# Second layer by seven products per pair: whole-block weight conversion and another order of products in a step

## The chip, the cores and the metric

The kernel runs on one core of one Trainium2 chip. The core has five engines that run side by side, each with its own queue worked off in order: PE (TensorE, matmuls into PSUM), DVE (VectorE), ACT (ScalarE), POOL (GpSimd), and SP (SyncE), which here only issues DMAs. The metric is the device time of one execution in microseconds (us); the median of several runs counts.

## What is computed

```
attn_out = _attn_ref(q, k, v)              # rotary attention, 2 x 8 heads, 576 x 64
x = attn_out as (1152 tokens, 512)
x = elu(x @ w_in) @ w_out                  # first layer,  512 -> 2048 -> 512
h = x @ w_in2                              # second layer, 512 -> 2048
g = h * tanh(log(1 + exp(h)))              # Mish
out = g @ w_out2                           # 2048 -> 512
```

The weights reach the chip in double precision (two 32-bit words per number) and are turned into single precision there. All matrix products are done in three parts: each operand is split into a high part and a low part, and high x high, low x high and high x low are summed.

## The kernel before

The change lies in the second layer alone (`second`, `pair_step`, `last_step`, `out_sum`). The 2048 hidden columns are 16 blocks of 128, taken as 8 pairs q = 0 to 7. Pair 0 is done the plain way (`classic`, three blocks of 384 tokens). For each later pair the first product (x @ w_in2) is done with seven half-size products instead of eight, numbered as in the table `P`: `x.mm(k)` issues product k, 12 matmuls of 288 columns. Products 1, 6, 7, 4 sum one after the other in PSUM bank "a", product 2 goes to bank "b", products 5 and 3 to bank "c"; between them ACT copies the bank's state out (`x.copy`), and DVE adds banks to the copies (`x.add`, L1068, and `x.add22`, L1072). `x.act` applies Mish and writes the high part of g (L1082, L1083, ACT), `x.lo` and `last_lo` the low part (L1086, DVE). The operands t1 to t4 of products 5, 6, 7, 4 are differences of token blocks, formed once at the layer's start on DVE (`form`, L886) and split by `put_hi` (ACT, L909) and `put_lo` (DVE, L913). Product 6 adds to what product 1 left in bank "a", so it can start only when ACT has copied "m1" out of it.

A step q (1 to 6, `pair_step`; 7, `last_step`) does four things at once:

- PE: the seven products of pair q, and nine output blocks (`out_mm`, L1122, six matmuls of 512 columns each) of pair q - 1. An output block goes to one of two PSUM buffers `ps_h`.
- DVE: nine sums (`out_sum`, L1132), each adding an output block to Y and freeing its buffer. For pair 0 it is ACT that copies the block to Y (L1130).
- Weights in: `w` is the two input blocks of pair q + 1, `o` the two output blocks of pair q, `on` those of pair q + 1. `load` makes ACT take the upper words (L92, a tile `wv` for input blocks, `wu` for output blocks); `bits` are three DVE operations (L103, L107, L111) that need the raw block; after the third the raw buffer is free. `w.sums` forms four differences of the input blocks (L820, DVE). `round` writes the high part on ACT and the low part on POOL (L116, L117), or on DVE where `nc.vector` is given.
- SP: DMAs of raw blocks (512 KB each, L78 and L83). There are three raw buffers. A load is issued as soon as the buffer that it takes is free; the buffers are handed out in the order in which their blocks' last bit operations stand in the program.

The order inside a step is written by hand: `pair_step` is a list of calls, and every engine works off its own part of it in that order. In the old list the three blocks `w[0]`, `o[0]`, `o[1]` are converted interleaved, then comes the first bit operation of `w[1]`, and only behind it the first three sums. PE's order is products 2, 1, 5, 6, three output blocks, products 7, 3, six output blocks, product 4.

Of the kernel before, what the change touches and what calls it, by code (L numbers as in the profile page):

```python
# [13 lines left out]
AF = mybir.ActivationFunctionType  # L14
# [11 lines left out]
def kernel(  # L26
# [11 lines left out]
    nc = tc.nc  # L38
# [812 lines left out]
    def moe(mp, early):  # L851
# [274 lines left out]
        def out_sum():  # L1126
            pair, t, o = banks.pop(0)
            y = Y.rearrange("p (t e) -> p t e", e=DM)[:, t, :]
            if pair.q == 0:
                nc.scalar.activation(out=y, in_=o, func=AF.Copy)  # L1130
            else:
                nc.vector.tensor_tensor(out=y, in0=y, in1=o, op=ALU.add)  # L1132
                if pair.q == NF // 2 - 1:
                    nc.sync.dma_start(out=out[t * 128:t * 128 + 128, :], in_=y)

        def pair_step(x, prev, w, o, on):
            x.mm(2)
            x.mm(1)
            x.mm(5)
            w.load(0)  # L1140
            prev.last_lo()
            x.copy("m1", "a")
            w.bits(0, 0)
            w.load(1)
            x.mm(6)
            out_mm()
            o[0].bits(0)
            out_mm()
            x.add("m1", "b")
            o[0].bits(1)  # L1150
            o[1].bits(0)
            w.bits(0, 1)
            x.copy("u2", "a")
            o[1].bits(1)
            w.bits(0, 2)
            o[1].bits(2)
            out_mm()
            o[0].bits(2)
            x.copy("m5", "c")
            w.bits(1, 0)  # L1160
            out_sum()
            out_sum()
            out_sum()
            x.mm(7)
            x.mm(3)
            o[0].round()
            out_mm()
            w.bits(1, 1)
            w.bits(1, 2)
            out_mm()  # L1170
            out_mm()
            x.copy("u3", "a")
            o[1].round(nc.vector)
            out_sum()
            x.add("u2", "c")
            x.act("m1")
            w.sums(0)
            w.sums(1)
            w.round(0)
            on[0].load()  # L1180
            out_mm()
            w.sums(2)
            out_mm()
            x.lo("m1")
            out_mm()
            out_sum()
            out_sum()
            w.round(1)
            w.sums(3)
            x.add22()  # L1190
            x.act("u2")
            out_sum()
            w.round(3)
            w.round(2)
            x.mm(4)
            out_sum()
            x.act("u3")
            out_sum()
            x.lo("u3")
            x.lo("u2")  # L1200
            x.act("s")
            on[1].load()

        def last_step(x, prev, o):
            prev.last_lo()
            x.mm(2)
            x.mm(1)
            x.copy("m1", "a")
            x.mm(5)
            o[0].bits(0)  # L1210
            o[0].bits(1)
            o[0].bits(2)
            o[0].round()
            x.copy("m5", "c")
            x.add("m1", "b")
            x.mm(6)
            x.copy("u2", "a")
            x.act("m1")
            out_mm()
            out_mm()  # L1220
            o[1].bits(0)
            out_sum()
            x.lo("m1")
            x.mm(3)
            out_sum()
            o[1].bits(1)
            o[1].bits(2)
            o[1].round(nc.vector)
            x.add("u2", "c")
            out_mm()  # L1230
            out_mm()
            x.act("u2")
            out_sum()
            out_sum()
            x.mm(7)
            x.lo("u2")
            x.copy("u3", "a")
            out_mm()
# [12 lines left out]
            out_mm()  # L1251
            out_sum()
            out_sum()

        def second():
            NQ = NF // 2
            x = Pair(0)
            w = ahead_pieces
            x.classic(0)
            w.round(0)  # L1260
            put_hi(0, "t4")
            form(1, "t3")
            form(1, "t2")
            x.classic_act(0)
            x.classic_hi(0)
            x.classic(1)
            w.sums(0, 1, 2, 3)
            w.round(1)
            put_hi(1, "t2")
            x.classic_lo(0)  # L1270
            form(0, "t1")
            form(1, "t1")
            x.classic_act(1)
            x.classic_hi(1)
            put_lo(1, "t2")
            w.round(2)
            x.classic(2)
            x.classic_lo(1)
            put_hi(1, "t3")
            w.round(3)  # L1280
            form(1, "t4")
            put_lo(0, "t4")
            put_hi(0, "t1")
            put_hi(1, "t1")
            put_lo(0, "t1")
            put_lo(1, "t1")
            x.classic_act(2)
            x.classic_hi(2)
            put_hi(1, "t4")
            put_lo(1, "t3")  # L1290
            o = [Block(NF + 2 + j) for j in range(2)]
            for b in o:
                b.load()
            put_lo(1, "t4")
            for q in range(1, NQ):
                prev, x = x, Pair(q)
                queue.extend((prev, t) for t in range(NT // 128))
                if q + 1 < NQ:
                    on = [Block(NF + 2 * q + 2 + j) for j in range(2)]
                    pair_step(x, prev, Pieces(q + 1), o, on)  # L1300
                    o = on
                else:
                    last_step(x, prev, o)
            queue.extend((x, t) for t in range(NT // 128))
            while queue:
                out_mm()
                out_sum()

        psum("ps_g")
        with tc.manual_schedule():  # L1310
# [13 lines left out]
            o = [(x[1:], g2_mm(*x[1:])) for x in pend[:1]]  # L1324
# [100 lines left out]
```

## Time and profile before

| | us |
|---|---|
| runs (3) | 595.06 median, 593.76 to 595.62 |
| profiled execution, time | 597.14 |
| profiled execution, span of the trace | 595.4 |
| PE busy | 551.8 (93%) |
| DVE busy | 426.7 (72%) |
| ACT busy | 313.6 (53%) |
| POOL busy | 226.9 (38%) |

The execution takes 1.74 us more than the span that the trace shows. Attention and the first layer fill the span to 351, pair 0 of the second layer runs to 363.65, and from there to 555.11 the six steps follow; the rest is the last step and the last nine output blocks. The profile's row of the granted PE clock shows 9 tenths or more until then and falls to 6 to 9 in the steps. Busy shares are means over stages with different limits: what the change is worth is read from the stage that it touches, there from the waits of PE.

### The profile page before, as it was taken

Reading aid. Unit: us, or ns where it says so; the run is one execution under the profiler, and the core shown is the slowest. Engines: PE = TensorE matmul, PEld = TensorE weight load, DVE = VectorE, ACT = ScalarE, POOL = GpSimd, SP = SyncE. Lnnn points to the kernel's source line nnn. Section 1 sums busy time; section 2 is a strip of 40 time slices with the busy share of each in tenths; the row PEclk is TensorE's granted clock in tenths of the full one; section 3 lists DMA queues with packets and bytes.
Section 4 is the critical chain, followed back from the end, with each engine's and each line's share of the span. In section 5 each row is a group of like instructions: output and inputs, shape, how many; then the busy total and the mean of one; then the engine's idle time right before and its main releaser. Section 6 shows DMA issues by size and latency. Waiting matters only on the chain.

```text
span 595.4 us, 9057 instructions
## 1 busy us (share of the span) xinstructions
PE 551.8 (93%) x3390; PEld 496.7 (83%) x3390; DVE 426.7 (72%) x663; ACT 313.6 (53%) x557; POOL 226.9 (38%) x206
## 2 busy tenths in 40 slices
PE   7999999999999999999999999597979797888997
PEld 6678888888999999999999998486767677776985
DVE  4667777788879878898867889445656665666664
ACT  3666767686566655445555556282535352525430
POOL 7899998633254443444330112030303040302200
PEclk9999999999999999999999999698999989898999
DMA  8368888762323333233232110402121212111004
GB/s 257 102 166 217 214 211 216 183 176 83 107 70 108 107 107 106 72 106 106 73 105 70 37 36 0 141 1 106 36 107 35 106 37 89 54 61 46 1 0 160
DMA packets 49100, 59.81 MB, mean 100 GB/s; under 512 B 20768, under 2 KB 38944, under 8 KB 48288
## 3 DMA queue, kind: packets, MB, share of 16 engines
q1 hardware_dynamic: 48512, 58.64, 33.1%
q8 instruction: 27, 0.44, 0.3%
q10 hardware_dynamic: 544, 0.59, 0.3%
q14 instruction: 17, 0.14, 0.1%
HBM read 47.51 MB, written 2.36 MB: 84 GB/s over the span
## 4 chain that ended last, share of the span: by engine, by line
PE 66%; DVE 15%; DMA 8%; ACT 5%; issue 3%; POOL 2%; SPq 1%; ACTq 0%; DVEq 0%; POOLq 0%
PE ps_s L207 16%; PE ps_h L1122 13%; PE ps_g L922 13%; PE ps_s L1044 10%; PE ps_s L441 5%; PE psA L548 5%; DMA raw<-in_w_in_dram 4%; PE psT L508 3%; DMA qb<-ql 2%; DVE wu L107 2%; DMA v_t<-in_vp_dram 1%; DVE Y L1132 1%; DMA tab<-in_rope_dram 1%; DVE Y L936 1%; DVE ws L820 1%
## 5 line engine op out<-in xcount | busy, mean ns | idle before, releaser
L448 DVE TENSOR_REDUCE mn<-ps_s 128x1 f32<-128x576 f32 x72 | 53.7, 755 | 25.6 <-PE ps_s L441 24.6
L1132 DVE TENSOR_TENSOR Y<-Y,ps_h 128x512 f32<-128x512 f32 x63 | 42.3, 686 | 35.7 <-PE ps_h L1122 35.4
L1122 PE MATMUL ps_h<-wo0h,gg 128*128 128x512 f32 x144 | 47.6, 413 | 17.4 <-DVE Y L1132 10.1
L1122 PE MATMUL ps_h<-wo0bh,gg 128*128 128x512 f32 x144 | 47.8, 414 | 15.1 <-DVE Y L1132 15.1
L461 ACT ACTIVATE P<-ps_s,mn 128x576 f32<-128x576 f32 x72 | 53.0, 738 | 14.4 <-DVE mn L448 14.1
L1122 PEld LDWEIGHTS ps_h<-wo0h,gg 128*128 128x128 f32 x144 | 26.8, 194 | 25.3 <-DVE Y L1132 11.8
L1122 PEld LDWEIGHTS ps_h<-wo0bh,gg 128*128 128x128 f32 x144 | 27.2, 194 | 23.5 <-DVE Y L1132 17.8
L117 POOL TENSOR_TENSOR wo0l<-wu,wo0h 128x512 fp32r<-128x512 f32 x9 | 13.7, 1519 | 80.8 <-ACT wo0h L116 66.3
L508 PE MATMUL psT<-idn,P 128*128 128x128 f32 x288 | 43.0, 273 | 0.0
L117 POOL TENSOR_TENSOR wo0bl<-wu,wo0bh 128x512 fp32r<-128x512 f32 x8 | 11.7, 1462 | 77.9 <-ACT wo0bh L116 70.4
L107 DVE SCALAR_TENSOR_TENSOR wu<-raw,wu 128x512 int32<-128x512 int32 x50 | 40.2, 804 | 1.2
L528 ACT ACTIVATE pt<-psT 128x512 f32<-128x512 f32 x43 | 25.6, 595 | 22.6 <-PE psT L508 22.5
L548 PE MATMUL psA<-pt,v_t 128*64 128x256 f32 (+1 forms) x240 | 36.1, 401 | 0.6 <-ACT R L493 0.3
L111 DVE SCALAR_TENSOR_TENSOR wu<-raw,wu 128x512 int32<-128x512 int32 x50 | 35.6, 723 | 1.1
L508 PEld LDWEIGHTS psT<-idn,P 128*128 128x128 f32 x288 | 34.7, 141 | 1.9 <-issue 1.5
L254 DVE SCALAR_TENSOR_TENSOR tb<-ta,tb 128x768 f32<-128x768 f32 x22 | 21.5, 976 | 20.2 <-ACT tb L250 20.1
L92 ACT ACTIVATE wv<-raw 128x512 f32<-128x512 f32 x14 | 9.2, 659 | 46.2 <-DMA raw<-in_w_in_dram 46.2
L1064 ACT ACTIVATE ta<-ps_s 128x576 f32<-128x576 f32 x28 | 17.5, 646 | 30.4 <-PE ps_s L1044 30.3
L103 DVE TENSOR_SCALAR wu<-wu 128x512 int32<-128x512 int32 x50 | 31.4, 629 | 0.0
L207 PE MATMUL ps_s<-XH,wi0h 128*128 128x384 f32 x120 | 31.0, 338 | 0.0
L207 PE MATMUL ps_s<-XL,wi0h 128*128 128x384 f32 x120 | 30.6, 335 | 0.0
L207 PE MATMUL ps_s<-XH,wi0l 128*128 128x384 f32 x120 | 30.6, 335 | 0.0
(229 smaller groups left out, 1653.5 us busy)
## 6 DMA issues: line engine op xcount, KB each, us to landing
raw<-in_w_in_dram SPq DMA_DIRECT2D x32, 512.0 KB, 3.7
raw<-in_w_out_dram SPq DMA_DIRECT2D x32, 512.0 KB, 3.6
qk_t<-in_qk_dram SPq DMA_DIRECT2D x6, 1152.0 KB, 5.9
qa<-qh SPq DMA_DIRECT2D x24, 144.0 KB, 3.7
out_dram<-Y SPq DMA_DIRECT2D x9, 256.0 KB, 2.0
ka<-kh SPq DMA_DIRECT2D x12, 144.0 KB, 5.4
ka<-kl SPq DMA_DIRECT2D x12, 144.0 KB, 4.9
qb<-ql SPq DMA_DIRECT2D x12, 144.0 KB, 3.0
```

The source lines that it names most:

```text
L103: nc.vector.tensor_scalar(out=ui, in0=ui, scalar1=3, scalar2=0x7FFFFFF8, op0=ALU.logical_shift_left, op1=ALU.bitwise_and)
L107: nc.vector.scalar_tensor_tensor(out=ui, in0=high, scalar=-0x80000000, in1=ui, op0=ALU.bitwise_and, op1=ALU.bitwise_or)
L111: nc.vector.scalar_tensor_tensor(out=ui, in0=low, scalar=29, in1=ui, op0=ALU.logical_shift_right, op1=ALU.bitwise_or)
L207: nc.tensor.matmul(o[:, j, :CH], lhsT=ws[j][i][:, cc, :], rhs=x[:, cc, t * CH:t * CH + CH], start=(k == 0), stop=(k == 3 * NC - 1),)
L448: nc.vector.tensor_reduce(out=m, in_=psS[u][:, :, :HS], axis=AX.XY, op=ALU.min)
L461: nc.scalar.activation(out=P.rearrange("p (j n) -> p j n", j=2), in_=psS.pop(u)[:, :, :HS], func=AF.Exp, scale=-1.0, bias=mn_t.pop(u), acc ...
L508: nc.tensor.transpose(tv[:, c, :], P[:, k:k + 128], idn)
L548: nc.tensor.matmul(o[64 * h:64 * h + 64, cols], lhsT=v, rhs=rhs, start=(c == 0 and first), stop=(c == 4), skip_group_check=True,)
L922: nc.tensor.matmul(o[:, j, :CH], lhsT=WO[f][w][:, e * 128:e * 128 + 128], rhs=g_part(f, t, i), start=(k == 0), stop=(k == 3 * GF - 1),)
L1044: nc.tensor.matmul(self.o[r][:, u, :H2], lhsT=w[i][:, cc, :], rhs=XO[u][xn][x][:, cc, :], start=(first and n == 0), stop=(last and n == 3 ...
L1122: nc.tensor.matmul(o, lhsT=l, rhs=w, start=(k == 0), stop=(k == 5))
L1132: nc.vector.tensor_tensor(out=y, in0=y, in1=o, op=ALU.add)
```

## The change

- `pair_step` is written in another order. PE: products 1, 2, 6, three output blocks, products 7, 5, two output blocks, product 4, an output block, product 3, three output blocks. DVE: all bit operations of `o[0]` and `o[1]`, then three sums (an `add` between them), then all those of `w[0]` and `w[1]`. The Mish of product 4 (`x.act("s")`) stands before the rounding of `w`. `o[1].round` goes from DVE to POOL, `w.round(3)` (a half block) from POOL to DVE.
- `out_sum` copies pair 0's output blocks on DVE, not on ACT.
- `last_step`: `o[1].round` goes from DVE to POOL.
- `second`: the calls ahead of step 1 are in another order.

```diff
             if pair.q == 0:
-                nc.scalar.activation(out=y, in_=o, func=AF.Copy)
+                nc.vector.tensor_copy(out=y, in_=o)
...
         def pair_step(x, prev, w, o, on):
+            x.mm(1)
             x.mm(2)
-            x.mm(1)
...
-            o[1].round(nc.vector)
...
+            o[1].round()
...
+            w.round(3, nc.vector)
 
         def last_step(x, prev, o):
...
-            o[1].round(nc.vector)
+            o[1].round()
...
-            w.sums(0, 1, 2, 3)
-            w.round(1)
+            w.sums(0, 1, 2)
+            w.round(2)
             put_hi(1, "t2")
             x.classic_lo(0)
+            put_lo(1, "t2")
+            x.classic_act(1)
+            x.classic_hi(1)
+            w.sums(3)
             form(0, "t1")
             form(1, "t1")
-            x.classic_act(1)
-            x.classic_hi(1)
-            put_lo(1, "t2")
-            w.round(2)
+            put_hi(1, "t3")
             x.classic(2)
             x.classic_lo(1)
-            put_hi(1, "t3")
-            w.round(3)
+            w.round(1)
+            put_lo(1, "t3")
             form(1, "t4")
             put_lo(0, "t4")
+            w.round(3)
+            x.classic_act(2)
+            x.classic_hi(2)
             put_hi(0, "t1")
             put_hi(1, "t1")
             put_lo(0, "t1")
             put_lo(1, "t1")
-            x.classic_act(2)
-            x.classic_hi(2)
             put_hi(1, "t4")
-            put_lo(1, "t3")
```

DVE at the head of step 3, before (`gg<-sx` is the low part of the last Mish of the pair before, `wv` an input block, `wu` an output block, `Y<-Y,ps_h` a sum; rows that follow each other and read alike are one row with a count):

```order
L1086 TENSOR_TENSOR gg<-sx,gg 128x2x288
L103 TENSOR_SCALAR wv<-wv 128x512
L103 TENSOR_SCALAR wu<-wu 128x512
L1068 TENSOR_TENSOR ta<-ta,ps_s 128x576
L107 SCALAR_TENSOR_TENSOR wu<-raw,wu 128x512
L103 TENSOR_SCALAR wu<-wu 128x512
L107 SCALAR_TENSOR_TENSOR wv<-raw,wv 128x512
L107 SCALAR_TENSOR_TENSOR wu<-raw,wu 128x512
L111 SCALAR_TENSOR_TENSOR wv<-raw,wv 128x512
L111 SCALAR_TENSOR_TENSOR wu<-raw,wu 128x512 x2
L103 TENSOR_SCALAR wv<-wv 128x512
L1132 TENSOR_TENSOR Y<-Y,ps_h 128x512 x3
```

The same place in the changed kernel:

```order
L1086 TENSOR_TENSOR gg<-sx,gg 128x2x288
L103 TENSOR_SCALAR wu<-wu 128x512 x2
L107 SCALAR_TENSOR_TENSOR wu<-raw,wu 128x512
L111 SCALAR_TENSOR_TENSOR wu<-raw,wu 128x512
L107 SCALAR_TENSOR_TENSOR wu<-raw,wu 128x512
L111 SCALAR_TENSOR_TENSOR wu<-raw,wu 128x512
L1132 TENSOR_TENSOR Y<-Y,ps_h 128x512 x2
L1068 TENSOR_TENSOR ta<-ta,ps_s 128x576
L1132 TENSOR_TENSOR Y<-Y,ps_h 128x512
L103 TENSOR_SCALAR wv<-wv 128x512
L107 SCALAR_TENSOR_TENSOR wv<-raw,wv 128x512
L111 SCALAR_TENSOR_TENSOR wv<-raw,wv 128x512
```

The two output blocks are finished one by one, the three sums stand next, and both input blocks come behind the sums.

DVE in the second half of step 3, before (`ws` and the short `wv` rows are `w.sums`, `gg<-ta,gg` low parts of Mish results):

```order
L1132 TENSOR_TENSOR Y<-Y,ps_h 128x512
L1068 TENSOR_TENSOR ta<-ta,ps_s_4457 128x576
L820 TENSOR_TENSOR ws<-wv 128x256
L820 TENSOR_TENSOR wv<-wv 128x256
L820 TENSOR_TENSOR ws<-wv 128x256
L1086 TENSOR_TENSOR gg<-ta,gg 128x2x288
L1132 TENSOR_TENSOR Y<-Y,ps_h 128x512 x2
```

And in the changed kernel:

```order
L1132 TENSOR_TENSOR Y<-Y,ps_h 128x512
L820 TENSOR_TENSOR ws<-wv 128x256
L820 TENSOR_TENSOR wv<-wv 128x256
L820 TENSOR_TENSOR ws<-wv 128x256
L1086 TENSOR_TENSOR gg<-ta,gg 128x2x288
L1072 TENSOR_TENSOR ta<-ta 128x576
L820 TENSOR_TENSOR ws<-wv,ws 128x256
L1132 TENSOR_TENSOR Y<-Y,ps_h 128x512 x2
L1068 TENSOR_TENSOR ta<-ta,ps_s_4521 128x576
L1132 TENSOR_TENSOR Y<-Y,ps_h 128x512
```

DVE's work between the fourth sum and the next two stays of the same kind; on PE, product 3 now lies between the blocks that these sums serve.

ACT where pair 0 ends and step 1 begins, before (L1103 and L1106 are Mish and high part of pair 0, `XH` and `xt` the high parts of t1 and t4, `wu<-raw` and `wv<-raw` the loads, L1064 the copies of bank "a" and "c"):

```order
L909 ACTIVATE XH<-gg 128x2x288 x2
L1103 ACTIVATE ta<-ps_s 128x768
L1106 ACTIVATE gg<-ta 128x2x384
L909 ACTIVATE xt_3937<-gg 128x576
L92 ACTIVATE wu<-raw 128x512 x2
L92 ACTIVATE wv<-raw 128x512
L1064 ACTIVATE ta<-ps_s 128x576
```

And in the changed kernel:

```order
L1103 ACTIVATE ta<-ps_s 128x768
L1106 ACTIVATE gg<-ta 128x2x384
L909 ACTIVATE XH<-gg 128x2x288 x2
L909 ACTIVATE xt_3938<-gg 128x576
L92 ACTIVATE wu<-raw 128x512 x2
L1064 ACTIVATE ta<-ps_s 128x576 x2
L116 ACTIVATE wo0bh<-wu 128x512
```

The high parts of t1 moved behind pair 0's last Mish, the load of the first input block moved from before the first copy to behind the second.

## Rows read from the trace of the kernel before

**Rows 1.** Stages: bounds, length, busy by engine (PE, PEld, DVE, ACT, POOL), clock.
```profile
363.65:400.10 36.45, 27.74 (x139) 23.55 (x139) 20.82 (x32) 19.69 (x35) 7.41 (x7) 0.86 0.17 58
400.10:431.73 31.63, 26.58 (x140) 23.12 (x139) 19.61 (x35) 12.98 (x22) 6.06 (x5) 0.89 0.20 67
431.73:462.57 30.84, 25.81 (x140) 22.51 (x139) 19.36 (x34) 12.98 (x22) 6.05 (x5) 0.94 0.20 69
...
555.11:595.40 40.29, 36.48 (x194) 31.22 (x192) 22.45 (x34) 11.13 (x17) 1.35 (x1) 1.00 0.16 60
```

**Rows 2.** Timeline, PE, step 3: start, duration, what, count, idle before and its releaser.
```profile
431.73 0.43 PE L1044 MATMUL ps_s<-XH,wi1h 128*128 128x288 f32 x2
...
438.09 0.63 PE L1122 MATMUL ps_h<-wo0h,gg 128*128 128x512 f32 x2
...
440.65 0.40 PE L1122 MATMUL ps_h<-wo0l,gg 128*128 128x512 f32 x1
444.88 0.73 PE L1122 MATMUL ps_h<-wo0h,gg 128*128 128x512 f32 x2 [3.83 <-DVE Y L1132]
...
451.11 0.62 PE L1122 MATMUL ps_h<-wo0h,gg 128*128 128x512 f32 x2
...
453.90 0.63 PE L1122 MATMUL ps_h<-wo0h,gg 128*128 128x512 f32 x2
...
456.66 0.74 PE L1122 MATMUL ps_h<-wo0h,gg 128*128 128x512 f32 x2 [1.20 <-DVE Y L1132]
```

**Rows 3.** Stretches behind the first gaps: length, PE busy, granted clock, DMA share, GB/s.
```profile
413.30:418.40 5.10, 5.10 (x16) 0.50 0.03 9
...
444.90:449.30 4.40, 4.40 (x17) 0.61 0.03 10
```

**Rows 4.** Timeline, DVE, step 3, columns as in rows 2.
```profile
438.59 0.69 DVE L111 SCALAR_TENSOR_TENSOR wv<-raw,wv 128x512 int32<-128x512 int32 x1
439.19 1.29 DVE L111 SCALAR_TENSOR_TENSOR wu<-raw,wu 128x512 int32<-128x512 int32 x2
443.80 0.43 DVE L103 TENSOR_SCALAR wv<-wv 128x512 int32<-128x512 int32 x1 [3.32 <-ACT wv L92]
444.14 1.28 DVE L1132 TENSOR_TENSOR Y<-Y,ps_h 128x512 f32<-128x512 f32 x2
...
455.93 1.28 DVE L1132 TENSOR_TENSOR Y<-Y,ps_h 128x512 f32<-128x512 f32 x2
457.12 0.42 DVE L820 TENSOR_TENSOR ws<-wv,ws 128x256 f32<-128x256 f32 x1
```

**Rows 5.** Raw blocks in step 3: SP's issue, ACT's conversion, times from issue to landing.
```profile
439.34 0.38 SPq L78 DMA_DIRECT2D raw<-in_w_in_dram  x1
...
443.11 0.66 ACT L92 ACTIVATE wv<-raw 128x512 f32<-128x512 f32 x1 [7.36 <-DMA raw<-in_w_in_dram]
...
DMA to landing us min/median/max: 3.6/4.1/5.2
```

**Rows 6.** POOL's subtractions and DVE beside them, timeline.
```profile
355.41 1.54 POOL L117 TENSOR_TENSOR wi1l<-wv,wi1h 128x512 fp32r<-128x512 f32 x1 [18.52 <-ACT wi1h L116]
...
455.69 1.46 POOL L117 TENSOR_TENSOR wi0l<-wv,wi0h 128x512 fp32r<-128x512 f32 x1 [1.55 <-ACT wi0h L116]
...
355.72 1.85 DVE L886 TENSOR_TENSOR gg<-Y 128x576 f32<-128x576 f32 x1
357.60 0.76 DVE L886 TENSOR_TENSOR gg<-gg,Y 128x576 f32<-128x576 f32 x1
```

**Rows 7.** Entry into step 1: PE's first matmuls, then ACT, timeline.
```profile
363.65 0.42 PE L1044 MATMUL ps_s<-XH,wi1h 128*128 128x288 f32 x2
...
367.29 0.69 ACT L909 ACTIVATE xt<-gg 128x576 fp32r<-128x576 f32 x1 [0.43 <-DVE gg L886]
367.88 1.22 ACT L92 ACTIVATE wu<-raw 128x512 f32<-128x512 f32 x2
...
369.57 0.62 ACT L1064 ACTIVATE ta<-ps_s 128x576 f32<-128x576 f32 x1
```

More of the change, by code (lines that the diff above doesn't have):

```diff
@@ L1136, in pair_step @@
         def pair_step(x, prev, w, o, on):
+            x.mm(1)
             x.mm(2)
-            x.mm(1)
-            x.mm(5)
-            w.load(0)
             prev.last_lo()
+            o[1].bits(0)
+            o[0].bits(0)
             x.copy("m1", "a")
-            w.bits(0, 0)
-            w.load(1)
+            o[0].bits(1)
+            o[0].bits(2)
+            o[1].bits(1)
+            o[1].bits(2)
             x.mm(6)
             out_mm()
-            o[0].bits(0)
+            x.copy("u2", "a")
@@ L1148, in pair_step @@
+            o[0].round()
             out_mm()
[L1149 to L1156, printed above, removed]
             out_mm()
-            o[0].bits(2)
-            x.copy("m5", "c")
-            w.bits(1, 0)
+            w.load(0)
+            x.mm(7)
+            x.mm(5)
             out_sum()
             out_sum()
+            x.add("m1", "b")
@@ L1163, in pair_step @@
             out_sum()
-            x.mm(7)
+            w.bits(0, 0)
+            o[1].round()
+            w.load(1)
+            w.bits(0, 1)
+            w.bits(0, 2)
+            x.copy("u3", "a")
+            out_mm()
+            w.bits(1, 0)
+            on[0].load()
+            w.bits(1, 1)
+            out_mm()
+            x.mm(4)
+            w.bits(1, 2)
+            out_sum()
+            w.sums(0)
+            x.copy("m5", "c")
+            out_mm()
+            w.sums(1)
             x.mm(3)
-            o[0].round()
@@ L1167, in pair_step @@
-            out_mm()
-            w.bits(1, 1)
-            w.bits(1, 2)
+            w.sums(2)
+            x.act("m1")
+            x.act("s")
             out_mm()
             out_mm()
-            x.copy("u3", "a")
-            o[1].round(nc.vector)
+            x.lo("m1")
+            x.add22()
+            out_mm()
+            w.round(2)
+            w.sums(3)
+            out_sum()
             out_sum()
             x.add("u2", "c")
-            x.act("m1")
-            w.sums(0)
-            w.sums(1)
+            out_sum()
@@ L1179, in pair_step @@
             w.round(0)
[L1180 to L1185, printed above, removed]
+            x.act("u3")
+            x.act("u2")
+            x.lo("u3")
+            x.lo("u2")
+            w.round(1)
+            on[1].load()
             out_sum()
             out_sum()
-            w.round(1)
[L1189 to L1192, printed above, removed]
-            w.round(3)
-            w.round(2)
@@ L1195, in pair_step @@
[L1195 to L1202, printed above, removed]
+            w.round(3, nc.vector)
         def last_step(x, prev, o):
@@ L1266, in second @@
             x.classic(1)
-            w.sums(0, 1, 2, 3)
-            w.round(1)
+            w.sums(0, 1, 2)
+            w.round(2)
             put_hi(1, "t2")
             x.classic_lo(0)
+            put_lo(1, "t2")
+            x.classic_act(1)
+            x.classic_hi(1)
+            w.sums(3)
             form(0, "t1")
             form(1, "t1")
-            x.classic_act(1)
-            x.classic_hi(1)
-            put_lo(1, "t2")
-            w.round(2)
+            put_hi(1, "t3")
             x.classic(2)
             x.classic_lo(1)
-            put_hi(1, "t3")
-            w.round(3)
+            w.round(1)
+            put_lo(1, "t3")
             form(1, "t4")
             put_lo(0, "t4")
+            w.round(3)
+            x.classic_act(2)
+            x.classic_hi(2)
             put_hi(0, "t1")
```

## Prediction

> **What bounds the kernel now.** I first cut the trace into the stages of the second layer: six steps (one per pair of weight blocks), then the last step with the tail [rows 1]. A step is 30.84 us, and steps 3 to 6 repeat it (431.73 to 555.11, 123.38 us for four); step 2 takes 31.63 us, step 1 takes 36.45 us. The last step and the tail take 40.29 us at clock 1.00, with PE busy 36.48 of them. In a repeated step no engine but PE comes near the length: DVE 19.36 us, ACT 12.98, POOL 6.05. So either PE's own work sets the step, or a wait of PE does.
>
> PE's own work comes from its timeline [rows 2]. Four products run from 431.73 to 438.09, so one is 6.36 / 4 = 1.59 us; two output blocks run from 451.11 to 453.90, so one is 1.395 us. A step has 7 products and 9 blocks: 7 x 1.59 + 9 x 1.395 = 11.13 + 12.56 = 23.69 us. A step of 30.84 us thus loses 7.15 us, and the same view shows where. The third block starts at 444.88, where 440.65 + 0.23 (a block's sixth) = 440.88 would have been possible: 4.00 us. The seventh starts at 456.66 instead of 453.90 + 1.395 = 455.30: 1.36 us. After the first gap the granted clock is 0.61 for 4.40 us [rows 3], that is 4.40 x 0.39 = 1.72 us; after the second gap no such stretch follows. Together 7.08 of 7.15.
>
> **Why PE waits.** Both gaps are ended by DVE's sum into Y. The two PSUM buffers of the output blocks are full, and the sums that would free one stand in DVE's queue behind the first bit operation on the second input block of the next pair, at 443.80 [rows 4]. That waits 3.32 us for ACT's conversion at 443.11, which waits for the block's DMA [rows 5]. The DMA was issued at 439.34, 0.06 us after 438.59 + 0.69 = 439.28, the last bit operation that frees a raw buffer: three blocks are converted interleaved, all raw buffers come free between 439.28 and 440.48, and the load starts only then. So the chain is bits, DMA, conversion, bits, sums, PE. The second gap is plain queueing: sums at 455.93 behind four other DVE operations.
>
> **What the change does to a step.** The blocks of this pair are now converted to the end at the head of the step, one after the other, then come three sums, then the two input blocks. I lay the new order out from the first product at t = 0, with durations of rows; a sum starts 0.2 us after its block, since the last matmul of a block at 440.65 ends at 441.05 where the next could have started at 440.88 [rows 2]. PE without a wait: products 1, 2, 6 to 4.8; blocks 1 to 3 to 8.95; products 7, 5 to 12.1; blocks 4, 5 to 14.9; product 4 to 16.5; block 6 to 17.9; product 3 to 19.5; blocks 7 to 9 to 23.7.
>
> DVE: bits of one block take 0.43 + 0.69 + 0.69 = 1.81 us. Even if the last two sums of the step before end only at t = 1.9 (below), a subtraction of 128x256 (0.42) and one of 128x576 (0.76 [rows 6]) bring it to 3.1, and the two output blocks to 3.1 + 2 x 1.81 = 6.7; the first raw buffer is free at about 5.2. The new load's landing takes 3.6 to 5.2 us [rows 5], so the second input block is there by 8.8 to 10.4 and converted by 11.1. Sums 1 and 2 (0.64 each) follow their blocks, at 6.7 and 7.8; the third block on PE needs the first sum by 7.56 and gets it at about 7.4. Sum 3 ends at 9.8, and the bits of the two input blocks follow: the first to 11.6, the second to 13.4. The second is wanted at 11.6, 0.5 us after the late case. Sum 4 at 13.8 serves block 6, wanted at 16.5. Then come four operations of 0.42 and two of 0.76, to 17.6; sums 5 and 6 end at 18.2 and 18.9 for blocks 7 and 8, which want them at 19.5 and 20.9; sum 7 ends at 21.8 for block 9, at 22.3. So every wait of PE for a sum ends 0.2 to 2 us early, the tightest at block 3. Both gaps and the clock loss go: the step is PE's 23.69 us, at clock 1.00 as in the last step.
>
> What is late next: weights for the next step. On ACT the Mish of product 4 now stands ahead of their rounding, which so starts at 18.0; POOL's two low parts of 1.46 us [rows 6] end near 21.5, and the next step's first product wants them with its fifth matmul, at 24.2: 2.7 us left. SP's four loads per step keep their order and each waits for its own buffer; 2 MB in 23.7 us is little.
>
> **POOL gets one more subtraction** (the second output block, 128x512, from DVE) and gives a half block to DVE. The trace shows what POOL costs DVE: the same 128x576 operation takes 1.85 us beside a POOL subtraction and 0.76 alone, while two sums beside POOL's 455.69 take 0.64 each [rows 4, 6]. In the new order POOL's 7 us fall on sums, except the last one (22.3 to 23.8), which meets the subtraction of u2. That is 1.1 us or so, delays sums 8 and 9 to t = 1.9 of the next step (used above) and costs nothing, since block 1 wants their buffers at 4.8. [...]
>
> **Step 1** starts at 363.65 and has its own trouble. Product 6 now comes third, at 363.65 + 2 x 1.59 = 366.83, and wants bank a copied by ACT. Ahead of that copy ACT has the high part of t4, which in the old trace starts at 367.29 once DVE has formed t4 [rows 7]. DVE now does one more low part (0.76) before that form: 368.05. Then 0.59 (to 367.88 in the old trace), two conversions of raw weights (1.22) and the copy (0.62): 370.48. PE waits 3.6 us. After the old first gap the clock fell, in step 3 for 1.72 us (0.61 over 4.40) and in step 2 for 2.55 us (0.50 over 5.10) [rows 3]; I take 2.1, with 0 as the other end. Step 1 is then 23.69 + 3.6 + 2.1 = 29.4 us. How often POOL holds DVE on the way to that form is open; a meeting is 1.85 - 0.76 = 1.09 us [rows 6]. Two fewer make the gap 1.4 us, after which, as after the 1.36 us, the clock need not fall: 25.1 us. One more makes it 4.7, with 2.55 of clock: 30.9 us. The nine copies of pair 0 move from ACT to DVE; no row shows such a copy on DVE, so it is 0 (hidden) to 0.64 (as a sum) each; DVE is busy 20.82 of 36.45 us in that step [rows 1]: 0.
>
> **Last step**: the second low part goes from DVE to POOL, a sum's 0.64 us or so off an engine that PE does not wait for there: 0. **The entry** (products of the first column, 351 to 363.65) keeps PE's instructions: 0.
>
> **Sum.** Step 1: 36.45 - 29.4 = 7.05. Step 2: 31.63 - 23.69 = 7.94. Steps 3 to 6: 123.38 - 94.76 = 28.62. Together 43.6 us off the span: 595.4 - 43.6 = 551.8. The profiled execution took 597.14, so 553.5 on its terms; the median of the runs, 595.06, lies 2.1 lower: 551.5.
>
> **Rivals.** *A gap per step stays.* DVE has slack of only 0.2 us at block 3 and 0.5 at the second input block; a slower DMA or another DVE wait bring one wait per step back. The old second gap prices it, 1.36 us without a fall of the clock, in six steps 8.2: 559.6. For: DVE is busy 19 of 23.7 us; against: a delay there moves into idle time further on.
> *Buffers still come free too late* (the change does not do what it says): the load lands after the sums want it, the 4.00 and 1.72 us stay and only the second gap goes, 6 x 1.36 = 8.2: 587. Against: the load's buffer is freed at 5.2 and the block wanted at 11.6.
> *Slower*: ACT's rounding, behind the Mish of product 4 and the low parts on POOL, comes too late for the next step's first product. In the old order the rounding did not stand behind the last product. It decides from 2.7 + 7.15 = 9.9 us of delay per step; at 10.5 us the step is 31.5, and the whole some 599. The longest wait that a row shows on that chain is 7.36 us [rows 5], and it is the one that the change attacks.
> *No change*: PE's clock or another engine takes the time back; nothing in the rows does, 595.
>
> **How the numbers follow.** Forecast 0.72, a gap per step 0.16, late buffers 0.05, slower 0.04, no change 0.03. The forecast's own span goes from 547.2 (step 1 at 25.1: 551.5 - 4.3) to 553.0 (at 30.9), and some way on towards the first rival; the range 547 to 560 takes that in and leaves out 0.12. Faster by over 0.3% (about what a measurement of this kernel can tell from no change, 1.8 us) 0.93, within it 0.03, slower 0.04.
>
> **What would show it.** Right: steps of 23.7 us, PE's clock 1.00 through steps 2 to 6, no wait of an output block on Y above 0.2 us; the second input block's DMA issued some 5 us into a step and ACT not waiting for it; one gap of 2 to 4 us in step 1 before product 6, ended by ACT. Wrong: a wait for DVE's Y in every step, ACT waiting for raw, or PE waiting at a step's first product for POOL's low part.

## The result and the profile after

The changed kernel takes 552.52 us (median of 4, 551.88 to 554.0) where the kernel before takes 595.0 us (median of 4 runs on the same chip): a ratio of 0.929, 95% interval 0.927 to 0.932. The prediction said 551.5 us, 547 to 560. The profiled execution took 551.88 us, with a span of 550.1 us against 595.4 before. Of all the runs below one is left out of its median, a run of the kernel with the loads early that took 877.59 us at a mean clock of 0.558.

The stages of the changed kernel, columns as in [rows 1] (the last two, there and below, are the share of DMA and its GB/s); step 3 (414.95 to 438.67, 23.72 us as step 2) is left out, and the row behind it holds steps 4 to 6:

```profile
363.17:391.23 28.06, 24.23 (x139) 21.21 (x139) 25.23 (x39) 18.02 (x30) 9.54 (x7) 1.00 0.24 76
391.23:414.95 23.72, 23.72 (x139) 21.27 (x138) 19.42 (x34) 13.11 (x22) 6.84 (x6) 1.00 0.28 89
...
438.67:509.83 71.16, 71.16 (x415) 63.81 (x414) 58.25 (x100) 39.37 (x66) 20.50 (x16) 1.00 0.26 82
509.83:550.10 40.27, 36.50 (x193) 31.24 (x191) 23.32 (x35) 9.11 (x14) 3.16 (x3) 0.99 0.16 60
```

Steps 2 to 6 are 23.72 us each, with PE busy for all of it (its busy time equals their length) at clock 1.00; the last step is as long as before. Only step 1 still loses time. PE's timeline from 363 on has two waits of more than 0.3 us, both there:

```profile
369.75 0.40 PE L1044 MATMUL ps_s<-ge,wi1h 128*128 128x288 f32 x1 [3.26 <-ACT ta L1064]
374.98 0.73 PE L1122 MATMUL ps_h<-wo0h,gg 128*128 128x512 f32 x2 [0.57 <-DVE Y L1130]
```

What answers to [rows 4 to 6] in step 2 (from 391.23) stands on DVE, ACT, SP and POOL like this:

```profile
397.58 0.69 DVE L1132 TENSOR_TENSOR Y<-Y,ps_h 128x512 f32<-128x512 f32 x1 [1.00 <-PE ps_h L1122]
398.98 0.69 DVE L1132 TENSOR_TENSOR Y<-Y,ps_h 128x512 f32<-128x512 f32 x1 [0.71 <-PE ps_h L1122]
...
402.77 0.42 DVE L103 TENSOR_SCALAR wv<-wv 128x512 int32<-128x512 int32 x1
...
408.17 0.42 DVE L820 TENSOR_TENSOR ws<-wv,ws 128x256 f32<-128x256 f32 x1
...
412.96 1.42 DVE L1086 TENSOR_TENSOR gg<-ta,gg 128x576 fp32r<-128x576 f32 x2
414.30 0.68 DVE L1132 TENSOR_TENSOR Y<-Y,ps_h 128x512 f32<-128x512 f32 x1
...
399.08 0.68 ACT L92 ACTIVATE wv<-raw 128x512 f32<-128x512 f32 x1 [0.65 <-DMA raw<-in_w_in_dram]
...
409.24 0.61 ACT L116 ACTIVATE wi1h<-ws 128x512 fp32r<-128x512 f32 x1
...
395.31 0.38 SPq L78 DMA_DIRECT2D raw<-in_w_in_dram  x1
...
410.00 1.30 POOL L117 TENSOR_TENSOR wi1l<-ws,wi1h 128x512 fp32r<-128x512 f32 x1 [9.95 <-ACT wi1h L116]
411.25 1.31 POOL L117 TENSOR_TENSOR wi1l<-wv,wi1h 128x512 fp32r<-128x512 f32 x1
...
413.82 1.71 POOL L117 TENSOR_TENSOR wi1l<-wv,wi1h 128x512 fp32r<-128x512 f32 x1 [1.25 <-ACT wi1h L116]
```

The first two sums now wait for PE (1.00 and 0.71 us), where before PE waited 3.83 us for them. The load of the second input block is issued at 395.31, 4.08 us into the step (before: 439.34, 7.61 us into step 3), its conversion at 399.08 waits 0.65 us for the DMA instead of 7.36, and its first bit operation at 402.77 waits for nothing.

### The profile page after: what moved, and what is told of

Same layout as the page of the kernel before. It is cut to its first block, busy times and chain, and to the rows that moved or that the text cites. A ratio compares the mean times of both kernels' runs of the same rounds, so it can differ in the third digit from the quotient of the medians.

```text
span 550.1 us, 9065 instructions
## 1 busy us (share of the span) xinstructions
PE 537.2 (98%) x3390; PEld 488.2 (89%) x3390; DVE 431.4 (78%) x671; ACT 310.0 (56%) x548; POOL 233.4 (42%) x207
## 4 chain that ended last, share of the span: by engine, by line
PE 80%; DVE 9%; ACT 3%; POOL 3%; issue 2%; DMA 2%; SPq 0%; ACTq 0%; POOLq 0%; DVEq 0%
PE ps_h L1122 18%; PE ps_s L207 17%; PE ps_g L922 14%; PE ps_s L1044 13%; PE ps_s L441 7%; PE psA L548 6%; PE psT L508 4%; DMA tab<-in_rope_dram 1%; DVE Y L936 1%; DVE gg L886 1%; DVE mn L448 1%; DVE wu L111 1%; ACT XH L938 1%; DVE XL L942 1%; DMA qb<-ql 1%
## 5 line engine op out<-in xcount | busy, mean ns | idle before, releaser
L1122 PE MATMUL ps_h<-wo0h,gg 128*128 128x512 f32 x144 | 45.3, 396 | 0.6 <-DVE Y L1130 0.6
L1122 PE MATMUL ps_h<-wo0bh,gg 128*128 128x512 f32 x144 | 45.2, 395 | 0.0
L1064 ACT ACTIVATE ta<-ps_s 128x576 f32<-128x576 f32 x28 | 18.3, 652 | 46.3 <-PE ps_s L1044 46.3
L117 POOL TENSOR_TENSOR wo0l<-wu,wo0h 128x512 fp32r<-128x512 f32 x12 | 17.5, 1469 | 50.8 <-ACT wo0h L116 50.8
L117 POOL TENSOR_TENSOR wo0bl<-wu,wo0bh 128x512 fp32r<-128x512 f32 x12 | 17.1, 1443 | 46.5 <-ACT wo0bh L116 40.3
L103 DVE TENSOR_SCALAR wu<-wu 128x512 int32<-128x512 int32 x50 | 31.9, 649 | 0.0
L117 POOL TENSOR_TENSOR wi0l<-wu,wi0h 128x512 fp32r<-128x512 f32 x10 | 14.9, 1493 | 35.7 <-ACT wi0h L116 35.7
```

The costliest lines, as they stand in the source:

```text
L117: (by or nc.gpsimd).tensor_tensor(out=lo, in0=u, in1=plain(hi), op=ALU.subtract)
```

## The experiments

My theory: two causes cost a step its 7 us, the late raw load and DVE's order around the sums, the clock adds to the first, and the order of the products takes away the second wait. The main rivals: the load alone, or DVE's order alone, is all of it. Each run is set beside runs of the kernel before on the same chip.

**The sums ahead of the conversion, loads as late as before**

```diff
--- the kernel before, pair_step
             x.copy("m5", "c")
-            w.bits(1, 0)
             out_sum()
             out_sum()
             out_sum()
+            w.bits(1, 0)
             x.mm(7)
```

> The kernel before with one edit: the conversion of the first block of the second raw input buffer goes behind the three sums that free the output tile's banks, instead of ahead of them, on VectorE. The raw loads start as late as before. Theory A (two causes: the late raw load and the order on VectorE each cost something by itself): the wait of 3.83 us ahead of the output product shrinks, but the copy of u2 on ScalarE still stands behind the late conversion, so some 2 us appear ahead of product 7, the clock stays up and the second wait of 1.36 us remains: a step of about 27.2 us, the whole about 576 us (570 to 582). Theory B (the order on VectorE alone is the cause): only the second wait is left, a step of about 25.2 us, the whole about 566 us. Theory C (the late raw load alone): nothing moves, 593 to 596 us.

Measured: 577.82 us, ratio 0.970 (0.968 to 0.972). Theory A held. Step 2 of this kernel, PE's waits and ACT's conversion:

```profile
411.90 0.40 PE L1044 MATMUL ps_s<-ge,wi0h 128*128 128x288 f32 x1 [1.64 <-ACT ta L1064]
420.74 0.74 PE L1122 MATMUL ps_h<-wo0bh,gg 128*128 128x512 f32 x2 [1.20 <-DVE Y L1132]
...
410.65 0.66 ACT L92 ACTIVATE wv<-raw 128x512 f32<-128x512 f32 x1 [7.44 <-DMA raw<-in_w_in_dram]
```

The wait for Y ahead of the third block is gone, but ACT still stands 7.44 us at its conversion, and the copy that product 7 wants stands behind it: 1.64 us. The second wait is untouched. The granted clock is 1.00 through the whole of step 2, which is 27.47 us long; four more steps with the same two waits follow (1.51 to 1.66 us and 1.18 to 1.20). So the late load costs PE time by a second way too, over ACT's queue.

**The loads early, products and sums as before**

```diff
--- the kernel before, pair_step
-            w.bits(0, 0)
+            o[0].bits(0)
+            o[0].bits(1)
+            o[0].bits(2)
+            o[1].bits(0)
+            o[1].bits(1)
+            o[1].bits(2)
...
+            w.bits(0, 0)
             w.bits(0, 1)
...
```

(Where lines are left out, the old places of the bit operations of `o` are taken away.)

> The kernel before with the other half of the change alone: the six conversions of the output blocks stand first, and then those of the input buffer, block by block, so that each raw buffer comes free in one piece and its load starts some 4 us earlier; the order of the products and the place of the second input buffer's conversion ahead of the three sums stay. Theory A (the late raw load is most of it): the data are there when VectorE comes to them, the first wait falls from 3.83 to 0.7 to 1.0 us, the clock stays up, the second wait of 1.36 us stays: a step of 25.8 us, the whole about 567 us (562 to 572). Theory B (the order on VectorE alone): the sums still stand behind the conversion, so the first wait stays above 3 us and the whole at 585 us or more.

Measured: 567.98 us (three runs), ratio 0.954 (0.952 to 0.956). Theory A held; a step is 25.85 us. In step 2 of this kernel (from 396.46), PE, DVE, ACT and SP:

```profile
406.18 0.73 PE L1122 MATMUL ps_h<-wo0bh,gg 128*128 128x512 f32 x2 [0.40 <-DVE Y L1132]
416.41 0.73 PE L1122 MATMUL ps_h<-wo0bh,gg 128*128 128x512 f32 x2 [1.20 <-DVE Y L1132]
...
405.09 0.43 DVE L103 TENSOR_SCALAR wv<-wv 128x512 int32<-128x512 int32 x1 [0.23 <-ACT wv L92]
...
404.37 0.69 ACT L92 ACTIVATE wv<-raw 128x512 f32<-128x512 f32 x1 [3.90 <-DMA raw<-in_w_in_dram]
...
400.68 0.38 SPq L78 DMA_DIRECT2D raw<-in_w_in_dram  x1
```

With the load issued 4.22 us into the step the first wait shrinks to 0.40, although the sums still stand behind the conversion of the second input block. Early loads alone bring 27.2 of the 42.5 us; the second wait of 1.20 stays.

**The changed kernel with the conversion ahead of the sums again**

```diff
--- the changed kernel, pair_step
             w.load(0)
+            o[1].round()
+            w.load(1)
+            w.bits(1, 0)
             x.mm(7)
             x.mm(5)
             out_sum()
             out_sum()
             x.add("m1", "b")
             out_sum()
             w.bits(0, 0)
-            o[1].round()
-            w.load(1)
...
-            w.bits(1, 0)
```

> The changed kernel with the rounding of the second output block, the load of the second input buffer and the conversion of that buffer's first block put ahead of the three sums of the output tile again. The raw loads start as early as in the changed kernel. Theory A (early load and sums ahead are both needed): the sums come behind a conversion whose data land at 7.9 us of the step, later than the first sum's end at 7.4, so the output products wait about 2.1 us in each of five steps: about 566 us (560 to 570), with the clock up. Theory B (the time of the load is all that mattered): within 1 us of the changed kernel, 552 to 553.5 us.

Measured: 574.88 us, ratio 0.965 (0.963 to 0.967): the wait is the one that theory A expected, the time is 9 us more. In step 2 (from 394.31), DVE and ACT, and then, with the columns of [rows 1], four stretches from the wait on and a whole later step:

```profile
403.01 0.43 DVE L103 TENSOR_SCALAR wv<-wv 128x512 int32<-128x512 int32 x1 [3.34 <-ACT wv L92]
403.35 1.28 DVE L1132 TENSOR_TENSOR Y<-Y,ps_h 128x512 f32<-128x512 f32 x2
...
402.31 0.66 ACT L92 ACTIVATE wv<-raw 128x512 f32<-128x512 f32 x1 [0.80 <-DMA raw<-in_w_in_dram]
```

```profile
402.03:404.09 2.06, 0.00 (x1) 0.01 (x1) 1.08 (x3) 0.66 (x1) 1.05 (x1) 1.00 0.50 189
404.09:405.70 1.61, 1.61 (x7) 1.29 (x8) 1.20 (x2) 0.00 (x0) 0.00 (x0) 0.92 0.00 0
405.70:408.57 2.87, 2.87 (x13) 2.87 (x12) 2.57 (x5) 0.00 (x0) 0.00 (x0) 0.50 0.00 0
408.57:411.00 2.43, 2.43 (x17) 2.30 (x17) 1.14 (x2) 1.71 (x3) 0.00 (x0) 0.94 0.66 189
...
421.88:449.39 27.51, 25.50 (x139) 22.61 (x138) 19.24 (x34) 13.09 (x22) 6.79 (x6) 0.94 0.25 77
```

The conversion at 402.31 (8.0 us into the step) holds the sums, and PE waits 2.06 us. Behind the wait the clock falls: 1.61 x 0.08 + 2.87 x 0.50 + 2.43 x 0.06 = 1.71 us more. 23.72 + 2.06 + 1.71 = 27.49, against a measured 27.57 (27.51 in step 3, the last row). So the place of the sums is worth 3.8 us a step even with the loads early; rival B is out. I had assumed that the clock stays up after a wait of 2 us; in all five of these steps it falls, after 2.00 to 2.11 us. The rest of the 22 us to the changed kernel lies in step 1, 31.67 us long.

**The changed kernel with the old order of products**

```diff
--- the changed kernel, pair_step
-            x.mm(1)
             x.mm(2)
+            x.mm(1)
+            x.mm(5)
...
             x.copy("u2", "a")
+            x.copy("m5", "c")
...
             x.mm(7)
-            x.mm(5)
+            x.mm(3)
...
-            x.mm(4)
...
-            x.copy("m5", "c")
...
-            x.mm(3)
...
-            x.act("s")
...
+            x.mm(4)
             w.round(1)
...
+            x.act("s")
```

> The changed kernel with the order of the seven products in a step as before (product 5 ahead of 6, product 3 ahead of 4, product 4 last) and the copy of product 5 and the Mish of the sum at the places that this order wants; conversions and loads as in the changed kernel. Theory A (the order of the products is worth the second wait): sums 4 and 5 come late to the bank that the seventh output block wants, one wait of about 2.4 us in a step: 26.1 us a step, the whole about 565 us (560 to 568). Theory B (the order of the products is worth nothing once the loads are early): 552 to 553.5 us.

Measured: 572.8 us, ratio 0.962 (0.960 to 0.965). The wait is there, at the seventh block; the time is 8 us above theory A and outside its range. Steps 2 and 3 (columns of [rows 1]), then PE, DVE and POOL at the wait in step 2:

```profile
393.46:421.48 28.02, 25.45 (x141) 22.30 (x139) 21.16 (x33) 13.10 (x22) 6.90 (x5) 0.94 0.25 75
421.48:448.04 26.56, 23.98 (x141) 21.18 (x139) 20.46 (x34) 13.10 (x22) 7.25 (x5) 1.00 0.25 80
```

```profile
414.11 1.22 PE L1122 MATMUL ps_h<-wo0bh,gg 128*128 128x512 f32 x2 [2.57 <-DVE Y L1132]
...
411.97 1.49 DVE L820 TENSOR_TENSOR ws<-wv,ws 128x256 f32<-128x256 f32 x1
413.38 1.27 DVE L1132 TENSOR_TENSOR Y<-Y,ps_h 128x512 f32<-128x512 f32 x2
...
411.53 1.65 POOL L117 TENSOR_TENSOR wi1l<-ws,wi1h 128x512 fp32r<-128x512 f32 x1 [7.13 <-ACT wi1h L116]
```

Without product 3 between them PE reaches block 7 before DVE has done the sums at 413.38. They are late by two things: the queue, and a difference of 128x256 that takes 1.49 us beside POOL's subtraction, where the same operation takes 0.42 in the changed kernel (408.17). There it stands 16.94 us into the step and POOL begins at 18.77 (410.00), behind the Mish of product 4 and the rounding. Here it comes at 18.51, and POOL, without that Mish ahead of the rounding, at 18.07. That is 1.07 of the 2.57 us, so the run bundles the order of the products with that of the Mish. The clock falls after the wait in steps 2, 4 and 6 (0.94 as the mean of a step) and not in steps 3 and 5 (1.00), with a wait of 2.57 or 2.58 us each time: 1.5 us of difference between the two kinds of step. Step 1 is 30.84 us long, 2.8 more than in the changed kernel. This kernel has the loads early and the sums ahead, and is still 4.8 us slower than the one with the loads early alone (567.98), whose calls differ at other places too: with the old order of products the sums ahead did not pay.

**Low parts of the second output block on DVE again**

```diff
--- the changed kernel, pair_step and last_step
-            o[1].round()
+            o[1].round(nc.vector)
```

> The changed kernel with the low parts of the second output block made by VectorE again instead of GpSimd, in all steps. It asks whether VectorE's time is tight in the steps that are 23.70 us long, with TensorE busy for 100% of them and VectorE for 19.40. Theory A (no: 4.3 us of a step are free on VectorE): the steps stay 23.7 us, the whole within 0.7 us of the changed kernel; step 1, where VectorE is busy for 25.2 of 28.1 us, may lose up to 0.7 us. Theory B (VectorE's queue has no slack at the sums, as the slack of 0.2 us in my sum has it): the 0.76 us of this work come out at TensorE in each step, some 4 us, 556 to 557 us.

Measured: 552.12 us, ratio 0.927 (0.925 to 0.928); the changed kernel beside it 552.36. Theory A held. Step 2, columns of [rows 1]:

```profile
390.65:414.37 23.72, 23.72 (x139) 21.27 (x138) 19.84 (x35) 13.11 (x22) 5.58 (x5) 1.00 0.29 89
```

DVE's busy time rises by 0.42 us in that step, and PE sees nothing of it. Step 1 is 28.09 us long. That edit is worth nothing that these runs can show, in either direction.

**The changed kernel once more**

> The changed kernel once more, as the measure for the runs beside it on the same chip: 552.5 us (551.5 to 554).

Measured: 552.36 us (552.17 to 553.1, 5 runs). Steps 2 to 6 are as in the first trace (118.60 us); step 1 differs. The stretches behind PE's wait there:

```profile
369.55:371.00 1.45, 1.45 (x10) 1.45 (x11) 1.45 (x4) 0.00 (x0) 0.00 (x0) 0.94 0.00 0
371.00:373.00 2.00, 2.00 (x8) 1.71 (x7) 1.93 (x5) 0.83 (x2) 0.00 (x0) 0.50 0.00 0
373.00:375.00 2.00, 2.00 (x8) 1.57 (x7) 1.70 (x3) 1.65 (x3) 1.47 (x1) 0.69 0.41 85
```

After a wait of 3.31 us ahead of product 6 the clock falls to one half here, after one of 3.26 us in the first trace it does not (1.00 over the whole of step 1). The loss is 1.45 x 0.06 + 2.00 x 0.50 + 2.00 x 0.31 = 1.71 us, but the slower PE then meets no wait at the third block (0.57 in the first trace). Step 1 is 28.83 us here and 28.06 there.

**Step 1: the high part of t4 ahead, copies left alone**

```diff
--- the changed kernel, pair_step (second loses the last four calls)
             x.mm(2)
+            if x.q == 1:
+                x.copy("m1", "a")
+                put_hi(1, "t4")
+                o[0].load()
+                o[1].load()
+                put_lo(1, "t4")
             prev.last_lo()
             o[1].bits(0)
             o[0].bits(0)
-            x.copy("m1", "a")
+            if x.q > 1:
+                x.copy("m1", "a")
```

> The changed kernel with the first half of that re-ordering: the high part of t4 and its loads go ahead, the six copies stay on VectorE behind the conversions. Theory A (each wait has a queue of its own): the wait ahead of product 6 falls from 3.42 to about 0.6 us, but TensorE then reaches the third output block at an earlier time and waits there for the first copy, which does not move: about 3.5 us there instead of 0.74, the whole within 0.7 us of the changed kernel (552 to 552.8 us). Theory B (the wait ahead of product 6 is all that step 1 loses): the whole falls by 2.8 us, to 549.7 us.

Measured: 554.45 us, ratio 0.930 (0.928 to 0.931), 2 us above the changed kernel beside it. Step 1 is 29.57 us. PE's one long wait, then stretches of step 1:

```profile
374.49 1.22 PE L1122 MATMUL ps_h<-wo0h,gg 128*128 128x512 f32 x2 [3.52 <-DVE Y L1130]
```

```profile
370.90:374.49 3.59, 0.07 (x2) 0.01 (x1) 3.49 (x7) 1.81 (x3) 1.25 (x1) 0.98 0.15 28
374.49:376.00 1.51, 1.51 (x4) 1.22 (x5) 1.20 (x2) 0.00 (x1) 1.51 (x2) 0.50 0.96 326
376.00:378.00 2.00, 2.00 (x9) 1.71 (x8) 0.55 (x1) 0.68 (x1) 0.19 (x1) 0.56 0.64 227
```

The wait ahead of product 6 is down to 0.31 us, but PE then stands 3.52 us at the third block, as theory A has it: the first copy of the output tile stands on DVE behind the six bit operations. What theory A did not have is the clock, 1.51 x 0.50 + 2.00 x 0.44 = 1.64 us behind the wait. The profiled execution, 552.88 us at a mean clock of 0.997, is the fastest of the four; the other three had 0.992 to 0.993 and took 554.2 to 554.7. Rival B (549.7) is out.

**Step 1: and two copies on ACT**

```diff
--- the kernel of the run above
-            if pair.q == 0:
+            if pair.q == 0 and t < 2:
+                nc.scalar.activation(out=y, in_=o, func=AF.Copy)
+            elif pair.q == 0:
                 nc.vector.tensor_copy(out=y, in_=o)
...
             x.copy("u2", "a")
-            o[0].round()
+            if x.q == 1:
+                out_sum()
             out_mm()
+            if x.q == 1:
+                out_sum()
+            o[0].round()
...
             x.mm(5)
-            out_sum()
-            out_sum()
+            if x.q > 1:
+                out_sum()
+                out_sum()
```

> The changed kernel with its first step alone re-ordered: copy of product 1, then the high part of t4 and its two loads, go ahead of the other work of VectorE and ScalarE, and the first two of the six copies of the output tile go from VectorE to ScalarE, ahead of the rounding of the first output block there. Theory A (the 3.42 us ahead of product 6 and the 0.74 us ahead of the third output block are two waits with causes of their own, both on queues): the first falls to about 0.6 us, the second to nothing, step 1 takes 24.5 to 25 us instead of 28.06, the whole 549 us (548.3 to 550), a ratio of 0.994 to the changed kernel. Theory B (the engines' work in step 1, 25.2 us of VectorE, is the bound, and the wait only moves): step 1 stays above 27 us, 551.5 to 553 us.

(The output tile has nine copies, not six.) Measured: 549.83 us, ratio 0.9226 (0.9213 to 0.9238), against 0.927 (0.9257 to 0.9282) for the changed kernel beside it: 2.5 us less. Step 1 is 26.69 us, between the two theories. PE's waits, then DVE and POOL ahead of the last one:

```profile
366.27 0.40 PE L1044 MATMUL ps_s<-ge,wi1h 128*128 128x288 f32 x1 [0.31 <-ACT ta L1064]
380.41 0.73 PE L1122 MATMUL ps_h<-wo0h,gg 128*128 128x512 f32 x2 [0.50 <-DVE Y L1132]
385.03 0.73 PE L1122 MATMUL ps_h<-wo0h,gg 128*128 128x512 f32 x2 [1.37 <-DVE Y L1132]
...
382.86 1.52 DVE L820 TENSOR_TENSOR ws<-wv,ws 128x256 f32<-128x256 f32 x1
...
382.66 1.43 POOL L117 TENSOR_TENSOR wi0l<-ws,wi0h 128x512 fp32r<-128x512 f32 x1 [6.44 <-ACT wi0h L116]
```

The waits ahead of product 6 and the third block are gone, and PE, some 3 us earlier, now catches up with DVE further on; 1.52 - 0.42 = 1.10 of the 1.37 us is again the difference held beside POOL. The 0.50 us ahead of block 6 goes back to POOL too: the copy that ends it stands behind the bit operations, of which L103 at 375.00 took 1.50 us beside POOL instead of 0.42.

**Step 1: and two more copies on ACT**

```diff
--- the kernel of the run above
-            if pair.q == 0 and t < 2:
+            if pair.q == 0 and t in (0, 1, 3, 4):
...
             w.bits(1, 0)
+            if x.q == 1:
+                out_sum()
             on[0].load()
...
             w.sums(3)
-            out_sum()
+            if x.q > 1:
+                out_sum()
             out_sum()
```

> The kernel of the run with two copies on ScalarE, with two more of the nine copies of the first output tile (output blocks 4 and 5) moved from VectorE to ScalarE in step 1, each right behind the output block that it reads. That run's step 1 was 26.69 us, with three waits on TensorE: 0.31 us ahead of product 6, 0.50 ahead of output block 6 and 1.37 ahead of output block 7, the last two ended by VectorE's copies of blocks 4 and 5, which stood behind its conversions and sums. Theory A (these two waits are a matter of VectorE's queue alone): both go, step 1 takes 24.7 to 25.0 us, the whole 547.9 us (547.4 to 548.6), a ratio of about 0.919 to the kernel before. Theory B (ScalarE, which then carries 2.4 us more than in the changed kernel in step 1, becomes late with its loads and rounds): a wait of 1 us or more shows at another place, and the whole stays at 549.5 us or above.

Measured: 547.94 us (median of 6, 547.58 to 550.44), ratio 0.921 (0.918 to 0.924). Theory A held: step 1 is 24.35 us, with one wait of 0.31 left. The ratio overlaps that of the kernel with two copies on ACT (0.9213 to 0.9238), so this last gain of 2.3 us is shown by the length of step 1 and not by the ratios. Step 1, columns of [rows 1]:

```profile
362.59:386.94 24.35, 24.04 (x139) 21.23 (x139) 23.45 (x34) 18.85 (x33) 8.43 (x6) 1.00 0.29 87
```

This kernel beats the changed one: 4.4 us by the medians (of two chips), and a ratio to the kernel before of 0.921 against 0.927, with intervals that do not meet. ACT takes four copies without a wait for PE, and DVE's busy time in step 1 falls from 25.23 to 23.45 us.

The length of a step, put together (the idle time ahead of the waiting matmul as its row has it, what the clock takes, and the step, in us; a row leaves out some 0.2 us of a gap, as 3.83 for 4.00 in [rows 2], and shorter waits are not listed, so a line does not quite add up). Each line is step 2, that of the kernel before step 3, that of the old products steps 2 and 3:

| kernel | first wait | second wait | clock | step |
|---|---|---|---|---|
| before | 3.83 | 1.20 | 1.72 | 30.84 |
| sums ahead | 1.64, at product 7 | 1.20 | 0 | 27.47 |
| loads early | 0.40 | 1.20 | 0 | 25.85 |
| changed, conversion ahead of sums | 2.06 | 0 | 1.71 | 27.57 |
| changed, old products | 0 | 2.57 | 1.5 or 0 | 28.02 or 26.56 |
| changed | 0 | 0 | 0 | 23.72 |

## Why the prediction was right, point by point

*Steps 2 to 6.* Right in size and cause. PE's own work of 23.69 us is what a step takes, 23.72. The load was freed at 4.08 instead of 5.2 and converted by 399.08 + 0.68, 8.5 us into the step instead of 11.1: my late case did not occur. The first sum ends 7.04 us into the step, said 7.4, wanted 7.56. The rounding begins 18.01 us in (said 18.0), and POOL's first two low parts end at 411.25 + 1.31, 21.3 us in (said 21.5).

That both halves of the reordering are needed was only implied in the sum, and it is now shown: loads alone leave 25.85 us, sums alone 27.47, and the changed kernel without its sums ahead has 27.57. That the new order of products is needed too is shown less cleanly: the one run with the old order moves the Mish as well, and none has the new order alone. The rivals "a gap per step stays" and "buffers still late" did not come, but the runs that bring one wait back show that my price of the former, 1.36 us without the clock, was too low: two waits of 2.06 and 2.57 us cost 3.8 and 2.8 to 4.3.

*POOL beside DVE.* I had POOL's last subtraction meet the low part of u2 for 1.1 us. It did not: the two low parts from 412.96 take 1.42 together, 0.71 each, the second from about 413.67 on, before POOL begins at 413.82, and the sum at 414.30 beside it takes 0.68. So sums are not held by POOL, as I had it, while a difference with both operands in SBUF is (1.49 for 0.42). The Trainium skill, "SBUF — State Buffer", section "Who interferes with whom", has a VectorE operation with two SBUF inputs contend with a GpSimd one that reads SBUF, and one with at most one SBUF input not, unless it runs in a mode that uses both ports; the rows of the sums and of the difference agree with it. One SBUF input alone is not enough to be free of POOL, as a bit operation in the kernel with four copies on ACT shows, DVE first:

```profile
374.93 1.51 DVE L103 TENSOR_SCALAR wv<-wv 128x512 int32<-128x512 int32 x1
...
374.87 1.28 POOL L117 TENSOR_TENSOR wo0bl<-wu,wo0bh 128x512 fp32r<-128x512 f32 x1
```

It reads one tensor and takes 1.51 us beside POOL, for 0.42 alone (402.77 above), as one does in the changed kernel at 514.55; whether it runs in such a mode no row shows. What I did not see is how much the place of the Mish does here: with the order of the products it keeps POOL off DVE's differences, 1.07 us of the wait that comes back with the old order.

*Step 1.* The wait ahead of product 6 was said to be 3.6 us and is 369.75 - (363.17 + 2 x 1.59) = 3.40, by the chain that I named. How often POOL holds DVE on the way there I had left open: twice (the low part L1110 at 363.39 takes 2.05 us for 0.94, L913 at 365.37 takes 1.29 for 0.74), as in the kernel before (L886 1.86 for 0.75, L913 1.30 for 0.75). DVE forms t4 at 366.58, and on ACT the high part and the copy stand like this:

```profile
367.36 0.68 ACT L909 ACTIVATE xt<-gg 128x576 fp32r<-128x576 f32 x1 [1.15 <-DVE gg L886]
367.95 1.21 ACT L92 ACTIVATE wu<-raw 128x512 f32<-128x512 f32 x2
369.06 0.63 ACT L1064 ACTIVATE ta<-ps_s 128x576 f32<-128x576 f32 x1
```

Two terms of the sum were mis-sized. The clock after it, taken at 2.1 us, is 0 in the first trace and 1.71 in the second, and the loss is partly time in which PE would have waited anyway. The nine copies on DVE, taken at 0, cost 0.74 us at the third block: the first copy starts only at 374.24, behind the bit operations. I had looked at DVE's busy share of the stage and not at what stands ahead of the first copy. Together 28.06 instead of 29.4; the two errors have opposite signs.

What step 1 lost in the kernel before (36.45 us) I did not take apart. Its long wait is at the third block, for ACT's copy to Y:

```profile
381.74 1.22 PE L1122 MATMUL ps_h<-wo0h,gg 128*128 128x512 f32 x2 [6.57 <-ACT Y L1130]
```

That copy stands on ACT behind the conversion of a raw block, which waits 9.26 us for its DMA, and behind two bank copies. With the loads early alone the wait is 4.14 us, with the sums ahead alone 6.49. No run moves the nine copies to DVE alone, and four of them back on ACT, each right behind its output block, cost no wait: what counted is what stands ahead of a copy, on ACT here and on DVE where it made PE wait 3.52 us.

*The rest.* The stage starts at 363.17, not 363.65. The start moves by as much without the change: the two kernels made from the kernel before by an edit in `pair_step` start it at 363.27 and 362.49. The last step is 40.27 (said 40.29). With 0.15 us more for the steps, the span of 551.8 in my sum becomes 551.8 - 1.34 - 0.48 + 0.13 = 550.1. I then took 2.1 us off because the profiled execution before lay that far above its median. Here the profiled execution lies 0.6 below its median (551.88 against 552.52), so that correction was chance, not a property of the kernel; without it, with 1.74 us outside the span, my sum stood at 553.5. That 551.5 comes out only 1 us below the median is thus in part luck: errors of both signs cancel.

## What to carry to other kernels

Where an engine's queue waits for a DMA, look for the operation that frees the DMA's buffer first, and then for what stands behind the waiting one: moving either alone left a wait (25.85 and 27.47 us), moving both, with an order of products that fits, gave PE's own time (23.72), and both with the old order of products were slower than the loads alone. When a step is bound by one engine's own work, lay every other engine's order out against it instruction by instruction, first of all at the start of a phase: a wait that is removed can show up at the next thing standing late in a queue, as the 3.3 us that moved from product 6 to the third block, and goes only when that is moved too. And a wait of the matmul engine of some 2 us or more can cost 1.5 to 3 us more in clock, so price it with 0 and with that.

## What the runs showed of the hardware

The granted clock does not follow from the length of the wait ahead of it alone. In the second layer of these traces it stayed at 1.00 after every wait of 1.70 us and less, and fell to 0.50 (1.2 of 2.4 GHz) at every wait of 3.52 us and more. Between them it did either. It fell after 1.96 us in step 1 of the kernel with the old products, and after 2.00 to 2.11 us in each of five steps of the one with the conversion ahead of the sums. After 2.57 or 2.58 us it fell in three steps of the kernel with the old products and not in the two between them, nor in its step 1. Of four waits of 3.26 to 3.31 us ahead of product 6 in step 1, each in a trace of its own, it fell after two (3.27 and 3.31) and not after the others (3.26 and 3.28). Where it fell, the loss was 1.5 to 1.7 us in the steps of the table and in the stretches of step 1 shown above, 2.55 in step 2 of the kernel before [rows 3], and more in step 1 of two kernels: 6.76 us at 0.59 with the conversion ahead of the sums, 7.26 us at 0.59 in the kernel before, 2.8 and 3.0 us. What decides between the two is not settled by these runs.
